# One decode-attention kernel: a V transfer in one piece, eight spare matmuls ahead of each wait for V, and one select for a mask

## The chip, the cores and the metric

The kernel runs on one core of one Trainium2 chip. The metric is the device time of one execution in microseconds (us); where several runs are given, the median counts.

## What is computed

Attention for one query per head: 16 heads, a cache of 8192 positions, 256 numbers each, all in bf16.

```python
B, H, Sq, Sk, D = 1, 16, 1, 8192, 256
scale = q.shape[-1] ** -0.5
scores = jnp.einsum("bhqd,bhkd->bhqk", q, k) * scale
p = _softmax(scores, axis=-1)
return jnp.einsum("bhqk,bhkd->bhqd", p, v)
```

Every number of K and V is used once.

## The kernel before, in words

**Tiles.** Heads go in pairs, eight of them, numbered 0 to 7. Each head takes 64 of the 128 partitions, so a partition holds J = 128 positions of its head. K of a pair is one tile of 128 x 32768 numbers, in two alternating buffers (`kbuf`); V is the same size in a single buffer (`vbuf`). Columns 0 to 63 are the first side of a pair (HJ = 64), the rest the second.

**Transfers.** SyncE issues all loads of K and V, in the order of the list `ORDER` (line 17), through one queue (line 136). A name without a plus is a whole tile, or the first half where `parts` (line 100) says so; with a plus it is the second half. The last V, v7, is cut at columns 64, 92, 112 and 124 (`CUTS`). Before a K transfer into a used buffer SyncE waits until the scores of the pair two before are done (line 125, 126); before a V transfer that ends within the first half it waits for the semaphore `pa`, the first 32 matmuls on the V before, else for `pr`, all of them (line 128). Behind the last piece it waits for its landing (line 139), then writes the outputs out (lines 143, 145).

**Scores.** Of each side's 64 positions GpSimd multiplies 24 with the query, three at a time (line 215), and ScalarE scales and sums them (line 450); VectorE does the other 40 (line 252). ScalarE reports each group of three on the semaphore `sp`: 16 groups (NG) for a pair, and the count starts two ahead.

**Softmax and V.** TensorE's program is a loop of nine passes, h = 0 to 8 (line 356). Pass h first does V of pair h - 1: it waits for the exponentials (`ex`, line 359), then for V (`v`, line 360), and multiplies with V two positions at a time (`doubles`, line 319), 32 matmuls for the first half and 32 for the second, behind a wait for `vb` (line 362); these take turns on two halves of the array's columns. In the last pass the second half stops at position 92: 46 matmuls in all. `total` (line 307) sums the exponentials and raises `pr`. Then pass h turns the maximum of pair h (line 292, a wait for VectorE's `m`), spreads it (line 296), and broadcasts the query of the pair after next (line 283). At its end the old `keep_running` multiplies the fp32 unit matrix by itself four times side by side, 128 x 512 in all, into a bank that nobody reads (line 330); then `gather` (line 341) waits for ScalarE's copy of the accumulator (`cm`, line 423) and joins the parts of pair h - 1.

ScalarE does, within the scores of the following pair, the exponentials (line 409), then the copy (line 423), and after the second side the final scaling (line 430). VectorE takes the maximum (line 234) behind the first side of the following pair.

**The end.** Behind the loop 72 small matmuls (line 384) add positions 92 to 127 of the last pair, in three groups that wait for the pieces of v7 at 92, 112 and 124. Then ScalarE and VectorE scale one half each (lines 471, 272).

**The start.** GpSimd builds the masks: `which`, two rows that are one over their head's 64 columns (one memset and two selects, lines 181 to 183), and `ident`, the unit matrix (lines 187, 188). TensorE needs `which` for its first two matmuls.

Of the kernel before, what the change touches and what calls it, by code (L numbers as in the profile page):

```python
# [5 lines left out]
ALU = mybir.AluOpType  # L6
# [7 lines left out]
GRP = 3  # L14
CH = 8
SIDES = 2
ORDER = "k0 k0+ k1 v0 k2 v1 k3 v2 k4 v3 k5 v4 k6 k6+ k7 v5 v5+ k7+ v6 v6+ v7"
CUTS = (0, 64, 92, 112, 124)
LAST_PAIRED = 92
STRIP = 64  # L20
BLK = 32
ROWS = 98
# [3 lines left out]
def bass_standalone__mha_softmax__decode_kernel(nc: bass.Bass, q: bass.AP, k: bass.AP, v: bass.AP, out: bass.AP):  # L26
    B, H, Sq, D = q.shape
    Sk = k.shape[2]
    P = 128
# [20 lines left out]
    with contextlib.ExitStack() as ctx:  # L50
# [9 lines left out]
        def sem(name):  # L60
            if name not in sems:
                sems[name] = ctx.enter_context(nc.semaphore(name))
            return sems[name]
# [33 lines left out]
        spare = ps("spare", [P, 512])  # L97

        stream = []
        parts = {name: (0, HJ) for name in ("k0", "k6", "k7", "v5", "v6")}  # L100
        for name in ORDER.split():
            kind, n = name[0], int(name[1])
            if name == f"v{LAST}":
# [56 lines left out]
        def _(pool):  # L160
            done = [0]

            def step(ins):
                done[0] += 1
                ins.then_inc(sem("pool"), 1)
                pool.wait_ge(sem("pool"), done[0])

            def keep(t, base, step_p, step_x, op, fill):
                step(
                    pool.affine_select(  # L170
                        out=t[:, :],
                        in_=t[:, :],
                        compare_op=op,
                        fill=fill,
                        base=base,
                        pattern=[[step_x, P]],
                        channel_multiplier=step_p,
                    )
                )

            step(pool.memset(which[:, :], 1.0))
            keep(which, 0, -HP, 1, ALU.is_ge, 0.0)
            keep(which, HP - 1, HP, -1, ALU.is_ge, 0.0)
            pool.nop().then_inc(sem("cb"), 1)
            for name, n in AHEAD.items():
                pool.nop().then_inc(sem(name), n)
            step(pool.memset(ident[:, :], 0.0))
            keep(ident, 0, 1, -1, ALU.not_equal, 1.0)
            step(pool.memset(ones, 1.0))
            step(pool.memset(half[:, :], 1.0))  # L190
            for c in (0, BLK):
# [89 lines left out]
        def _(pe):  # L281
# [45 lines left out]
                return ins  # L327

            def keep_running():
                pe.matmul(  # L330
                    spare[:, :].rearrange("p (b x) -> p b x", x=P),
                    lhsT=ident[:, :],
                    rhs=ident[:, :].rearrange("p (b x) -> p b x", b=1).to_broadcast([P, 512 // P, P]),
                    start=True,
                    stop=True,
                )

            def gather():
                for n in range(2):
# [16 lines left out]
            with pe.Fori(0, NP + 1) as h:  # L356
                par = pe.snap(h % 2)
                with pe.If(h > 0):
                    pe.wait_ge(sem("ex"), h)
                    pe.wait_ge(sem("v"), h * 16)  # L360
                    doubles(0, HJ).then_inc(sem("pa"), 1)
                    pe.wait_ge(sem("vb"), (h // (NP - 2) + h // LAST + h // NP) * 16 + 16)
                    doubles(HJ, LP)
                    with pe.If(h < NP):
                        doubles(LP, J)
                    total(h)
                with pe.If(h < NP):
                    pe.wait_ge(sem("m"), h + 1)
                    turned()
                    pe.wait_ge(sem("g"), h + 1)  # L370
                    spread()
                with pe.If(h < NP - 2):
                    qcast(back(h, -2), par)
                with pe.If(h > 0):
                    keep_running()
                    pe.wait_ge(sem("cm"), h)
                    pe.wait_ge(sem("fin"), h)
                    gather().then_inc(sem("pv"), 1)
# [124 lines left out]
```

## Time and profile before

| | us |
|---|---|
| median of 3 runs | 317.23 (317.05 to 317.38) |
| the profiled execution | 317.37 |
| its span, first to last instruction | 316.1 |
| VectorE busy | 225.6 (71%) |
| GpSimd busy | 209.8 (66%) |
| ScalarE busy | 194.6 (62%) |
| TensorE busy | 107.1 (34%) |
| mean granted TensorE clock | 0.73 of full |
| HBM read | 134.23 MB, 425 GB/s over the span |

The profiled execution has 1.27 us outside its span. Engines are named PE (TensorE matmul), PEld (its weight loads), DVE (VectorE), ACT (ScalarE), POOL (GpSimd), SP (SyncE); a q behind a name is the engine's sequencer. A timeline row holds start, duration, engine, line, operation, the tiles out<-in, the shape and the count, and in brackets the engine's idle time before it and what ended that. A row of a table of stages holds the stage, its length, the busy time and instructions of PE, PEld, DVE, ACT and POOL, the granted clock, the share of the DMA engines and GB/s. A row by line gives the shortest, median and longest duration in ns, and the first and last start.

### The profile page before, as it was taken

Reading aid. Unit: us, or ns where it says so; the run is one execution under the profiler, and the core shown is the slowest. Engines: PE = TensorE matmul, PEld = TensorE weight load, DVE = VectorE, ACT = ScalarE, POOL = GpSimd, SP = SyncE. Lnnn points to the kernel's source line nnn. Section 1 sums busy time; section 2 is a strip of 40 time slices with the busy share of each in tenths; the row PEclk is TensorE's granted clock in tenths of the full one; section 3 lists DMA queues with packets and bytes.
Section 4 is the critical chain, followed back from the end, with each engine's and each line's share of the span. In section 5 each row is a group of like instructions: output and inputs, shape, how many; then the busy total and the mean of one; then the engine's idle time right before and its main releaser. Section 6 shows DMA issues by size and latency. Waiting matters only on the chain.

```text
span 316.1 us, 7081 instructions
## 1 busy us (share of the span) xinstructions
PE 107.1 (34%) x718; PEld 46.8 (15%) x718; DVE 225.6 (71%) x1305; ACT 194.6 (62%) x840; POOL 209.8 (66%) x146
## 2 busy tenths in 40 slices
PE   0000000192005900069000790007700564258678
PEld 0000000041001400024000240002300122113335
DVE  0198989695596946969369692896989698969300
ACT  2066777766278653696537964468677967686541
POOL 3188888875486845858368582786888588868300
PEclk9999999997555785559755588555965558756779
DMA  8999999999999999999999999999999999999996
GB/s 333 402 460 456 473 398 398 489 440 398 398 398 531 398 398 398 531 398 398 489 440 398 398 531 398 398 398 464 398 464 398 464 398 464 398 464 406 456 400 267
DMA packets 3639, 134.25 MB, mean 425 GB/s; under 512 B 406, under 2 KB 438, under 8 KB 694
## 3 DMA queue, kind: packets, MB, share of 16 engines
q1 hardware_dynamic: 3620, 134.23, 98.8%
q8 instruction: 1, 0.02, 0.0%
q10 hardware_dynamic: 18, 0.01, 0.0%
HBM read 134.23 MB, written 0.01 MB: 425 GB/s over the span
## 4 chain that ended last, share of the span: by engine, by line
DMA 51%; POOL 16%; ACT 10%; PE 7%; issue 6%; ACTq 6%; POOLq 3%; SPq 0%
DMA kbuf<-in_k_dram 32%; DMA vbuf<-in_v_dram 19%; POOL prod L215 16%; ACT prod L450 8%; PE acc L319 6%; ACTq L450 4%; POOLq L215 2%; ACTq L446 2%; PE ob L384 1%; ACT E L409 0%; PE spare L330 0%; ACT comb L423 0%; POOLq L214 0%; POOLq L156 0%; POOLq L212 0%
## 5 line engine op out<-in xcount | busy, mean ns | idle before, releaser
L252 DVE SCALAR_TENSOR_TENSOR kbuf<-kbuf,qrow x640 | 219.9, 417 | 65.3 <-issue 65.3
L215 POOL TENSOR_TENSOR prod<-kbuf,q_now 128x768 f32 x128 | 207.0, 1639 | 83.5 <-ACT prod L450 46.3
L450 ACT ACTIVATE prod<-prod x384 | 155.3, 405 | 103.9 <-POOL prod L215 86.9
L319 PE MATMUL acc<-vbuf,E 128*64 128x512 bf16 x494 | 73.3, 468 | 15.7 <-DMA vbuf<-in_v_dram 12.7
L450 ACT ACTIVATION_READ_ACCUMULATOR prod<-prod x384 | 71.6, 186 | 0.0
L292 PE MATMUL mx<-ident,small 128*1 128x128 f32 x16 | 4.5, 380 | 176.2 <-DVE small L234 176.2
L252 DVE DVE_READ_ACCUMULATOR kbuf<-kbuf,qrow x640 | 52.8, 82 | 0.0
L319 PEld LDWEIGHTS acc<-vbuf,E 128*64 128x64 bf16 x494 | 33.0, 134 | 55.5 <-issue 25.8
L292 PEld LDWEIGHTS mx<-ident,small 128*1 128x1 f32 x16 | 0.7, 81 | 177.2 <-DVE small L234 177.2
L409 ACT ACTIVATE E<-S,negb 64x128 bf16 x16 | 13.9, 866 | 1.5 <-ACT negb L404 1.4
L330 PE MATMUL spare<-ident 128*128 128x512 f32 x16 | 14.7, 1016 | 0.1
L341 PE MATMUL ob<-comb,small 98*2 98x128 f32 x64 | 7.3, 373 | 9.9 <-ACT comb L423 9.9
L228 DVE RECIPROCAL small<-tot 34x1 f32 (+1 forms) x8 | 1.3, 159 | 10.8 <-PE tot L307 10.7
L423 ACT ACTIVATE comb<-acc 98x512 f32<-98x512 f32 x8 | 4.7, 593 | 6.2 <-PE tot L307 6.2
L409 ACT ACTIVATION_READ_ACCUMULATOR E<-S,negb 64x1 f32 x16 | 7.9, 494 | 0.0
L238 DVE TENSOR_REDUCE small<-mx 1x2 f32<-1x128 f32 x8 | 2.2, 279 | 7.0 <-PE mx L292 7.0
L341 PEld LDWEIGHTS ob<-comb,small 98*2 98x2 f32 x64 | 2.7, 99 | 22.0 <-ACT comb L423 21.0
L430 ACT ACTIVATE qo<-ob,small 2x128 f32 x14 | 4.9, 352 | 1.0 <-PE ob L341 0.9
L234 DVE TENSOR_REDUCE small<-S 128x1 f32 x8 | 2.3, 281 | 2.8 <-ACT prod L450 2.8
L296 PE MATMUL mx<-small 1*64 1x1 f32 x32 | 2.9, 244 | 3.0 <-DVE small L238 3.0
L330 PEld LDWEIGHTS spare<-ident 128*128 128x128 f32 x16 | 3.6, 279 | 1.4 <-issue 1.3
L283 PE MATMUL qrow<-qo,which 2*128 (+1 forms) x8 | 2.9, 391 | 2.6 <-DMA qo<-in_q_dram 2.4
(25 smaller groups left out, 19.9 us busy)
## 6 DMA issues: line engine op xcount, KB each, us to landing
kbuf<-in_k_dram SPq DMA_DIRECT2D x6, 4096.0 KB, 27.8
vbuf<-in_v_dram SPq DMA_DIRECT2D x5, 4096.0 KB, 23.7
vbuf<-in_v_dram SPq DMA_DIRECT2D x1, 1792.0 KB, 9.0
vbuf<-in_v_dram SPq DMA_DIRECT2D x1, 1280.0 KB, 11.7
vbuf<-in_v_dram SPq DMA_DIRECT2D x1, 768.0 KB, 13.1
vbuf<-in_v_dram SPq DMA_DIRECT2D x1, 256.0 KB, 13.3
kbuf<-in_k_dram SPq DMA_DIRECT2D x5, 44.1
vbuf<-in_v_dram SPq DMA_DIRECT2D x5, 27.9
```

The lines of the kernel that those rows point to most:

```text
L215: pool.tensor_tensor(out=prod[:, b * GRP * D : (b + 1) * GRP * D].rearrange("p (b d) -> p b d", b=GRP), in0=kbuf[:, ds(par * (J * D) + s * ...
L252: ins = dve.scalar_tensor_tensor(out=col, in0=col, scalar=SCALE, in1=qrow[:, ds(par * 512, D)], op0=ALU.mult, op1=ALU.mult, accum_out=S[:, ...
L292: pe.matmul(mx[0:1, 0:P], lhsT=m[:, :], rhs=ident[:, :], start=True, stop=True).then_inc(sem("mT"), 1)
L319: ins = pe.matmul(acc[at : at + STRIP, :], lhsT=E[:, x : x + STRIP], rhs=vbuf[:, j * D : (j + 2) * D], start=(j < 4), stop=(j >= J - 4), s ...
L330: pe.matmul(spare[:, :].rearrange("p (b x) -> p b x", x=P), lhsT=ident[:, :], rhs=ident[:, :].rearrange("p (b x) -> p b x", b=1).to_broadc ...
L341: ins = pe.matmul(ob[row : row + 2, 0:HW], lhsT=sel[:, 2 * n : 2 * n + 2], rhs=comb[:, n * D + a : n * D + a + HW], start=(n == 0), stop=( ...
L384: ins = pe.matmul(ob[row : row + 2, 0:HW], lhsT=E[:, at : at + 2], rhs=vbuf[:, j * D + a : j * D + a + HW], start=False, stop=(j == J - 1) ...
L409: ins = act.activation(out=E[rows, 0 : 2 * J].rearrange("p (b two i t) -> p b i two t", b=J // BLK, two=2, t=2)[:, :, :, :, x], in_=S[rows ...
L423: act.activation(out=comb[:, :], in_=acc[0:ROWS, :], func=ACT.Copy).then_inc(sem("cm"), 1)
L430: ins = act.activation(out=qo[:, ds(i * D + a, HW)], in_=ob[row : row + 2, 0:HW], func=ACT.Copy, scale=recip[row : row + 2, ds(i, 1)],)
L446: with act.Fori(0, SG) as i:
L450: ins = act.activation(out=part, in_=part, func=ACT.Copy, scale=SCALE, accum_out=S[:, ds(par * J + s * HJ + i * GRP + b, 1)],)
```

## The change

Three edits. GpSimd's two masks are built by one helper, a memset and one select each, so `which` takes one select instead of two. The sixth pair's V (pair 5, v5) goes in one transfer: `v5+` leaves the list, `v5` is the whole tile, and TensorE's wait for `vb` no longer counts it. And the spare product, one fp32 matmul ahead of `gather`, becomes a loop of eight bf16 matmuls of 512 columns (the fp32 ones read as pairs of bf16) between the wait for `ex` and that for `v`; in pass 6 TensorE there also waits until ScalarE has summed all groups of pairs 0 to 6.

```diff
-ORDER = "k0 k0+ k1 v0 k2 v1 k3 v2 k4 v3 k5 v4 k6 k6+ k7 v5 v5+ k7+ v6 v6+ v7"
+ORDER = "k0 k0+ k1 v0 k2 v1 k3 v2 k4 v3 k5 v4 k6 k6+ k7 v5 k7+ v6 v6+ v7"
+SPARES = 8
-        parts = {name: (0, HJ) for name in ("k0", "k6", "k7", "v5", "v6")}
+        parts = {name: (0, HJ) for name in ("k0", "k6", "k7", "v6")}
-            def keep(t, base, step_p, step_x, op, fill):
+            def ones_where_zero(t, pattern):
+                step(pool.memset(t[:, :], 0.0))
                 step(
                     pool.affine_select(
...
-            step(pool.memset(which[:, :], 1.0))
-            keep(which, 0, -HP, 1, ALU.is_ge, 0.0)
-            keep(which, HP - 1, HP, -1, ALU.is_ge, 0.0)
+            ones_where_zero(which, [[-1, 2], [0, HP]])
...
-            step(pool.memset(ident[:, :], 0.0))
-            keep(ident, 0, 1, -1, ALU.not_equal, 1.0)
+            ones_where_zero(ident, [[-1, P]])
...
             def keep_running():
-                pe.matmul(
-                    spare[:, :].rearrange("p (b x) -> p b x", x=P),
-                    lhsT=ident[:, :],
-                    rhs=ident[:, :].rearrange("p (b x) -> p b x", b=1).to_broadcast([P, 512 // P, P]),
-                    start=True,
-                    stop=True,
-                )
+                flat = ident[:, :].bitcast(BF16)
+                with pe.Fori(0, SPARES):
+                    pe.matmul(
+                        spare[:, :].rearrange("p (b x) -> p b x", x=2 * P),
+                        lhsT=flat[:, 0:P],
+                        rhs=flat.rearrange("p (b x) -> p b x", b=1).to_broadcast([P, 256 // P, 2 * P]),
+                        start=True,
+                        stop=True,
+                    )
...
                     pe.wait_ge(sem("ex"), h)
+                    with pe.If(h == NP - 2):
+                        pe.wait_ge(sem("sp"), (NP - 1) * NG + 2)
+                    keep_running()
                     pe.wait_ge(sem("v"), h * 16)
                     doubles(0, HJ).then_inc(sem("pa"), 1)
-                    pe.wait_ge(sem("vb"), (h // (NP - 2) + h // LAST + h // NP) * 16 + 16)
+                    pe.wait_ge(sem("vb"), (h // LAST + h // NP) * 16 + 16)
...
                 with pe.If(h > 0):
-                    keep_running()
                     pe.wait_ge(sem("cm"), h)
                     pe.wait_ge(sem("fin"), h)
                     gather().then_inc(sem("pv"), 1)
```

TensorE at the head of a pass of its loop, before: `acc` is the accumulator of the products with V, and the brackets name the semaphores that a row waits for.

```order
L358 COMPARE_AND_BRANCH
L360 REGISTER_ALU [waits ex]
L319 MATMUL acc<-vbuf,E 64x512 [waits v]
L319 MATMUL acc<-vbuf,E 64x512 x31
L362 ISA
L319 MATMUL acc<-vbuf,E 64x512 [waits vb]
```

The same place after:

```order
L359 COMPARE_AND_BRANCH
L361 COMPARE_AND_BRANCH [waits ex]
L361 UNCONDITIONAL_BRANCH [waits sp]
L330 UNCONDITIONAL_BRANCH
L331 MATMUL spare<-ident 128x512
L330 REGISTER_ALU
L330 COMPARE_AND_BRANCH
L364 REGISTER_ALU
L318 MATMUL acc<-vbuf,E 64x512 [waits v]
L318 MATMUL acc<-vbuf,E 64x512 x31
L366 ISA
L318 MATMUL acc<-vbuf,E 64x512 [waits vb]
```

A branch with the wait for `sp` (pass 6 alone takes it) and the loop of spare products now stand between the wait for `ex` and the first row that waits for V; the loop's three rows run eight times.

TensorE at the end of a pass and behind the loop, before: `ob` is the bank of the output rows.

```order
L372 UNCONDITIONAL_BRANCH
L374 COMPARE_AND_BRANCH
L330 MATMUL spare<-ident 128x512
L341 MATMUL ob<-comb,small 2x128 [waits fin,cm]
L341 MATMUL ob<-comb,small 2x128 x3
L374 UNCONDITIONAL_BRANCH
L356 REGISTER_ALU
L356 COMPARE_AND_BRANCH
```

After:

```order
L376 UNCONDITIONAL_BRANCH
L378 COMPARE_AND_BRANCH
L342 MATMUL ob<-comb,small 2x128 [waits fin,cm]
L342 MATMUL ob<-comb,small 2x128 x3
L378 UNCONDITIONAL_BRANCH
L357 REGISTER_ALU
L357 COMPARE_AND_BRANCH
```

The spare product ahead of the gather is gone; all else stands as it stood.

SyncE's transfers from the second half of pair 6's K on, before:

```order
L136 DMA kbuf<-in_k_dram 128x16384
L136 DMA kbuf<-in_k_dram 128x16384 [waits tp,kd]
L136 DMA vbuf<-in_v_dram 128x16384 [waits pa]
L136 DMA vbuf<-in_v_dram 128x16384 [waits pr]
L136 DMA kbuf<-in_k_dram 128x16384
L136 DMA vbuf<-in_v_dram 128x16384 [waits pa]
```

After:

```order
L137 DMA kbuf<-in_k_dram 128x16384
L137 DMA kbuf<-in_k_dram 128x16384 [waits tp,kd]
L137 DMA vbuf<-in_v_dram 128x32768 [waits pr]
L137 DMA kbuf<-in_k_dram 128x16384
L137 DMA vbuf<-in_v_dram 128x16384 [waits pa]
```

The two halves of v5, with a wait for `pa` and one for `pr`, have become one whole transfer that waits for `pr`.

More of the change, by code (lines that the diff above doesn't have):

```diff
@@ L172, in keep @@
                         in_=t[:, :],
[L173 to L177, printed above, removed]
-                    )
-                )
-            step(pool.memset(which[:, :], 1.0))
-            keep(which, 0, -HP, 1, ALU.is_ge, 0.0)
-            keep(which, HP - 1, HP, -1, ALU.is_ge, 0.0)
+                        compare_op=ALU.not_equal,
+                        fill=1.0,
+                        base=0,
+                        pattern=pattern,
+                        channel_multiplier=1,
+                    )
+                )
+            ones_where_zero(which, [[-1, 2], [0, HP]])
             pool.nop().then_inc(sem("cb"), 1)
```

## The prediction

> **What bounds the kernel now.** I read the page first, for the share of the DMA queue, then the chain of waits from 225 us on, then the timelines of single engines, and last the table of stages for the clock that TensorE was granted. The page's queue row:
>
> ```profile
> span 316.1 us, 7081 instructions
> ...
> q1 hardware_dynamic: 3620, 134.23, 98.8%
> ```
>
> All of K and V goes through one queue that moved data in 98.8% of the span. An engine's work matters only where it empties that queue, or behind the last bytes. What lies there is the end of the chain (start, duration, what):
>
> ```profile
> 291.18 12.97 DMA vbuf<-in_v_dram
> ...
> 304.20 6.71 PE acc L319 x46
> 310.91 0.04 PE tot L307 x2
> 310.95 1.05 PE spare L330 x2
> 312.00 0.54 PE ob L341 x8
> 312.54 2.03 PE ob L384 x72
> ```
>
> The last pair's first V half lands at 304.15 us, and from there TensorE works without a gap to 312.54 + 2.03 = 314.57. The queue of SyncE shows when the last V piece had landed, since line 143 stands behind line 139's wait for it:
>
> ```profile
> 314.08 0.32 SPq L143 DMA_DIRECT2D out_dram<-qo  x1
> ```
>
> So the last bytes came at 314.08, and 8 of the 72 matmuls of line 384 need them: 8/72 of 2.03 is 0.23 us, and the last drains in about 0.2. TensorE ends at 314.57, where the data alone would have ended it at about 314.5. Transfer and TensorE are level at the end: TensorE earlier gains under 0.1 us there, later it costs in full.
>
> How fast it is there hangs on its clock. The table of stages (length, busy us and instructions by engine, then the granted clock):
>
> ```profile
> 255.60:259.60 4.00, 3.97 (x20) 1.75 (x22) 4.00 (x25) 2.63 (x13) 3.23 (x2) 0.50 0.91 393
> 259.60:261.20 1.60, 1.60 (x16) 0.62 (x12) 1.60 (x11) 1.31 (x6) 1.40 (x1) 1.00 1.47 635
> 284.80:290.30 5.50, 5.50 (x26) 2.36 (x28) 5.50 (x35) 3.19 (x16) 4.97 (x4) 0.50 1.08 465
> 290.30:293.70 3.40, 0.84 (x8) 0.23 (x4) 3.40 (x21) 2.62 (x12) 2.88 (x2) 1.00 0.90 386
> 294.50:297.10 2.60, 2.60 (x14) 1.14 (x16) 0.00 (x0) 2.31 (x13) 0.86 (x1) 0.50 0.93 403
> 297.10:300.50 3.40, 2.95 (x30) 1.52 (x26) 0.72 (x3) 0.60 (x3) 0.00 (x0) 0.99 1.07 463
> 300.50:304.00 3.50, 1.72 (x10) 0.57 (x10) 0.00 (x0) 2.46 (x6) 0.00 (x0) 1.00 0.94 402
> 304.20:307.40 3.20, 3.20 (x16) 1.46 (x18) 0.00 (x0) 0.60 (x2) 0.00 (x0) 0.50 1.01 430
> 307.40:310.70 3.30, 3.30 (x32) 1.68 (x29) 0.00 (x0) 0.00 (x0) 0.00 (x0) 1.00 0.97 406
> ```
>
> Every burst on V starts at half clock and gets the full one later: 4.0, 5.5, 2.6 and 3.2 us after its start. The rates at both clocks:
>
> ```profile
> 304.20 1.07 PE L319 MATMUL acc<-vbuf,E 128*64 128x512 bf16 x4 [0.35 <-DMA vbuf<-in_v_dram]
> 307.72 1.24 PE L319 MATMUL acc<-vbuf,E 128*64 128x512 bf16 x10
> L319 PE MATMUL acc<-vbuf,E x494: 379/379/637, 63.0 to 310.5; 128*64 128x512 bf16 x165
> ```
>
> These matmuls go in pairs, one on each half of the array's columns. At half clock the second pair starts 1.07 - 0.64 = 0.43 us after the first; at full clock five pairs need four steps and one duration, so a step is (1.24 - 0.38)/4 = 0.215 us.
>
> **The change part by part.** *One select for rows.* GpSimd fills the mask of rows with one select fewer, and the unit matrix comes earlier:
>
> ```profile
> 1.07 0.63 POOL L170 TENSOR_SCALAR_AFFINE_SELECT which<-which 2x128 bf16<-2x128 bf16 x2
> 14.33 3.23 POOL L215 TENSOR_TENSOR prod<-kbuf,q_now 128x768 f32 x2 [9.54 <-issue]
> ```
>
> Half of 0.63 us goes, with GpSimd idle for 9.54 us before its first product at 14.33, which waits for K. Worth 0; without that cover it would be worth 0.3.
>
> *The sixth pair's V whole.* One issue instead of two, and TensorE starts on it when all of it is there. These TensorE rows hold the sixth and seventh pairs:
>
> ```profile
> 255.63 5.59 PE L319 MATMUL acc<-vbuf,E 128*64 128x512 bf16 x32 [4.04 <-DMA vbuf<-in_v_dram]
> 265.34 5.33 PE L319 MATMUL acc<-vbuf,E 128*64 128x512 bf16 x32 [4.12 <-DMA vbuf<-in_v_dram]
> 277.37 0.59 PE L292 MATMUL mx<-ident,small 128*1 128x128 f32 x2 [6.66 <-DVE small L234]
> 284.78 6.37 PE L319 MATMUL acc<-vbuf,E 128*64 128x512 bf16 x32 [0.86 <-DMA vbuf<-in_v_dram]
> 294.48 4.94 PE L319 MATMUL acc<-vbuf,E 128*64 128x512 bf16 x32 [3.34 <-DMA vbuf<-in_v_dram]
> ```
>
> Two halves are 265.34 - 255.63 = 9.71 apart, so 19.42 for both. Whole transfers, from two K landings with four transfers between them:
>
> ```profile
> 75.90 44.08 DMA kbuf<-in_k_dram
> 153.08 44.30 DMA kbuf<-in_k_dram
> ```
>
> (197.38 - 119.98)/4 = 19.35 each: the whole one saves 0.07 us of the queue. Against it stands the late start. The new wait holds TensorE until ScalarE has summed all of pair 6 (counted from 0); its next work there is:
>
> ```profile
> 264.65 0.71 ACT L430 ACTIVATE qo<-ob,small 2x128 f32 x2
> ```
>
> Spare matmuls from about 264.7, at 0.43 each, end at 268.2; nothing else is queued that any engine needs before 277.37, where the maximum is late anyway. But SyncE's issue of the next V half waits for the first 32 matmuls. With the full clock at 2.6 to 5.5 us after 264.7, these end between 271.6 and 272.7. The queue runs dry when the K half ahead lands, 9.71 before 284.78, so at 275.07. The last output transfer, from issue at 314.97 to the end of the span, took under 1.15 us, so the data flows again by 273.9: hidden by 1.2 us, and each us beyond that would cost one.
>
> *The spare matmuls of the other passes.* Eight times 0.43 is 3.4 us ahead of each V. In passes 1 to 5 whole transfers of V are asked for early:
>
> ```profile
> vbuf<-in_v_dram SPq DMA_DIRECT2D x5, 27.9
> ```
>
> 27.9 us from issue to landing, 19.35 of them moving: 8.5 us in hand against 3.4, so nothing. In the seventh pass the burst that began at 284.78 begins up to 3.4 us later, near 288.2, with the full clock by then or soon, and ends between 291.8 and 292.4 instead of at 291.18, where the chain has SyncE's next issue; the queue has work until 284.78 + 9.71 - 0.04, near 294.4. With 1.15 us to flow that is hidden by 0.9 us; nothing again.
>
> *The spare matmuls of the last pass* are on the path. The exponentials are long done there, since TensorE comes from the gather that waits for ScalarE's copy behind them:
>
> ```profile
> 302.59 0.60 ACT L423 ACTIVATE comb<-acc 98x512 f32<-98x512 f32 x1
> 303.24 0.60 PE L341 MATMUL ob<-comb,small 98*2 98x128 f32 x8 [1.58 <-ACT comb L423]
> L356 PEldq ALU_OP  x9: 36/36/36, 60.0 to 311.6; - x9
> L356 PEldq COMPARE_BRANCH  x9: 76/209/217, 60.1 to 311.7; - x9
> 310.98 0.60 ACT L423 ACTIVATE comb<-acc 98x512 f32<-98x512 f32 x1 [6.17 <-PE tot L307]
> 311.93 0.60 PE L341 MATMUL ob<-comb,small 98*2 98x128 f32 x8
> ```
>
> So no hole is filled: the eight stand between 303.84 and a V that is there at 304.15. A loop turn adds 0.04 + 0.21 of sequencer time, under 0.43, so it hides. I start them at 304.2, with a branch more than now. Half clock: the stage row shows it from 304.0 already with the old spare in the hole, and now the hole is empty. No row has eight full-width bf16 matmuls; 512 columns at half clock take 0.43 in the nearest rows. The old fp32 product is the far end, at 2.06 us for two records in 278.72's group:
>
> ```profile
> 278.72 2.06 PE L330 MATMUL spare<-ident 128*128 128x512 f32 x2
> ```
>
> At 1.03 each the eight would cost 4.8 us more; I take 0.43, the same type and columns. Below it stands 0.215 at full clock.
>
> Sum: 304.2 + 8 x 0.43 = 307.64, full clock from about then; 23 pairs have 22 steps of 0.215 and one duration of 0.38, ending at 312.75 against 310.91, so +1.84. The old spare behind the total goes: the gather can start 0.05 after the copy (303.24 against 303.19), so at 311.63 instead of 311.93: -0.30. With -0.07 from the whole V: **+1.47 us**. The profiled execution took 317.37 for a span of 316.1 and lies 0.14 above the median, 317.23; from the median, 317.23 + 1.47 = **318.7 us**.
>
> **The rivals.** *The clock stays full (not slower).* If the spare matmuls of the pass before, or a shorter pause, keep the full clock to 304.2, eight take 8 x 0.215 = 1.72 us, and the burst ends at 305.92 + 4.73 + 0.38 = 311.03: +0.12 - 0.30 - 0.07, which is before the last bytes allow, so 317.2. The point that decides: each us by which the full clock comes before 307.64 gives back half a us, so by 306.0 the loss is under 0.63 us. For it: the pauses at 301.7 and 303.8 are short. Against: the clock fell at 304.0 after just these pauses, and the soonest rise in the rows is 2.6 us into a burst, so 306.8. The Trainium skill, "TensorE: Matmul & The Clock Gate", section "Why this matters for your kernels", says that the clock falls only with idle gaps of over some 3 us between bursts; by that rule this rival would hold. The row of 300.50 to 304.00 disagrees: 1.72 us busy, no gap over 1.6 us, and the next stage is at 0.50. Chance 0.14.
>
> *The clock comes late.* With the rise 5.5 us after 304.2, as in the stage from 284.80, five pairs more run at 0.43: +1.05, so 319.8. The unit matrix, read as bf16, is mostly zeros; did it not count as work, the burst itself would have to earn the clock, up to 320.5. Chance 0.14.
>
> *An early chain.* If the seventh burst leaves the clock full at 294.48, its second half ends 1.1 us sooner, the spares move forward with it, and about 0.7 remain: 318.0. I count it to the forecast.
>
> *The queue runs dry at 275.07*, if the wait and a half clock make the first 32 matmuls end after 274: 1 us for each. Chance 0.04, 319.5.
>
> **How the numbers follow.** Forecast with the early chain 0.65, late clock 0.14, dry queue 0.04: 0.83 slower, of which 0.03 may fall within the bound; full clock 0.14; some gain that no row shows 0.03. A difference of 0.2%, 0.63 us, is what this kernel's runs can tell. Faster by so much would need the last bytes sooner, and 0.07 is all that the transfers give: 0.03. Within: 0.17. Slower: 0.80. The range reaches from 317.1, with the full clock in it, to 319.8.
>
> **What would show it.** Right: eight spare matmuls from about 304.2 at steps of 0.43, clock 0.50 there; the last burst from about 307.6; the gather 0.7 us behind the total; the last bytes still near 314.0, and the last matmuls 1.5 us later than now, all their data waiting for them. Wrong: a clock of 1.00 at 304, or spares that start before 303, or a queue with a gap near 275 or 294.

## The result and the profile after

| | before | changed |
|---|---|---|
| median of 6 runs, us | 317.31 (316.79 to 318.15) | 320.15 (319.64 to 321.42) |
| ratio | | 1.0087 (95%: 1.0061 to 1.0114) |
| profiled execution, us | 317.37 | 320.25 |
| its span, us | 316.1 | 318.8 |

The change makes the kernel 2.84 us slower; 1.47 was forecast. The forecast had the sign and the last pass right; the measured median lies 0.35 us above its range.

First the queue of V and K on the page, and the queue of SyncE from 255 us on, in the changed kernel:

```profile
q1 hardware_dynamic: 3476, 134.23, 98.0%
```

```profile
271.68 30.55 SPq L137 DMA_DIRECT2D vbuf<-in_v_dram  x7
315.12 0.32 SPq L144 DMA_DIRECT2D out_dram<-qo  x1
```

The same two rows of the kernel before (the second stands in the prediction) begin at 261.26 and 314.08. So the first V half of pair 6 is asked for at 271.68, as the prediction had it (271.6 to 272.7), but the last bytes come at 315.12, 1.04 us later than before, where the prediction had them at 314.0. The page's 98.8% of 316.1 us and this 98.0% of 318.8 us are the same work, 312.4 us. Of the 2.7 us that came on top, 1.65 lie behind the last bytes, where the queue has nothing left to do, and 1.04 ahead of them, where it was empty or slow.

TensorE's timeline from the second half of pair 6's V on:

```profile
295.06 5.33 PE L318 MATMUL acc<-vbuf,E 128*64 128x512 bf16 x32 [3.84 <-DMA vbuf<-in_v_dram]
300.23 0.20 PE L306 MATMUL tot<-lsum,half 128*34 128x1 f32 x2
304.20 0.60 PE L342 MATMUL ob<-comb,small 98*2 98x128 f32 x8 [2.82 <-ACT comb L426]
305.20 3.55 PE L331 MATMUL spare<-ident 128*128 128x512 bf16 x8 [0.40 <-issue]
308.69 5.21 PE L318 MATMUL acc<-vbuf,E 128*64 128x512 bf16 x46
313.73 0.20 PE L306 MATMUL tot<-lsum,half 128*34 128x1 f32 x2
314.62 0.60 PE L342 MATMUL ob<-comb,small 98*2 98x128 f32 x8 [0.69 <-ACT comb L426]
315.05 2.18 PE L387 MATMUL ob<-vbuf,E 128*2 128x128 bf16 x72
```

And the table of stages for the same stretch, with the granted clock third from the right:

```profile
295.10:298.60 3.50, 3.50 (x18) 1.58 (x20) 0.29 (x1) 1.92 (x8) 0.00 (x0) 0.51 1.05 449
298.60:300.40 1.80, 1.80 (x21) 0.95 (x16) 0.00 (x0) 0.00 (x0) 0.00 (x0) 1.00 0.85 364
305.20:308.80 3.60, 3.60 (x10) 0.91 (x12) 0.00 (x0) 0.56 (x2) 0.00 (x0) 0.53 1.00 419
308.80:313.90 5.10, 5.10 (x48) 2.62 (x48) 0.00 (x0) 0.00 (x0) 0.00 (x0) 1.00 0.93 383
```

The last pass is what was forecast, moved 1 us to the right. Eight spare matmuls from 305.20 to 308.69 at half clock (3.49 us, forecast 3.44); the burst behind them at full clock (5.04 to the total's start, forecast 4.95); the gather 0.89 behind the total (forecast 0.88). What was not forecast stands ahead of it: the second half of pair 6's V lands at 295.02 instead of 294.44, and its burst gets the full clock 3.5 us after its start instead of 2.7. From burst to total that is 5.17 us instead of 4.78.

So the 2.7 us of the span are the forecast 1.47, and 1.23 more: 0.58 for the late landing, 0.07 that the whole V did not bring to this place, 0.39 for the clock in that burst, and 0.19 in four small differences of the last pass. The clock's share is a matter of phase (see the account of the prediction below). The late landing is the one with a cause to find.

### The profile page after: what moved, and what is told of

It is laid out like the page before. It is cut to its first block, busy times and chain, and to the rows that moved or that the text cites. A ratio compares the mean times of both kernels' runs of the same rounds, so it can differ in the third digit from the quotient of the medians.

```text
span 318.8 us, 7320 instructions
## 1 busy us (share of the span) xinstructions
PE 106.2 (33%) x766; PEld 45.2 (14%) x766; DVE 225.6 (71%) x1305; ACT 194.6 (61%) x840; POOL 209.6 (66%) x145
## 4 chain that ended last, share of the span: by engine, by line
DMA 38%; POOL 18%; ACT 13%; PE 9%; issue 9%; ACTq 9%; POOLq 4%; DVE 0%; SPq 0%
DMA kbuf<-in_k_dram 31%; POOL prod L214 18%; ACT prod L453 11%; DMA vbuf<-in_v_dram 6%; PE acc L318 5%; ACTq L453 5%; POOLq L214 3%; PE spare L331 2%; ACTq L449 2%; ACT comb L426 1%; PE ob L387 1%; ACT E L412 1%; POOLq L213 0%; PE ob L342 0%; POOLq L157 0%
## 5 line engine op out<-in xcount | busy, mean ns | idle before, releaser
L318 PE MATMUL acc<-vbuf,E 128*64 128x512 bf16 x494 | 59.3, 400 | 3.8 <-DMA vbuf<-in_v_dram 3.8
L331 PE MATMUL spare<-ident 128*128 128x512 bf16 x64 | 28.1, 613 | 17.1 <-ACT prod L453 13.5
L318 PEld LDWEIGHTS acc<-vbuf,E 128*64 128x64 bf16 x494 | 28.4, 116 | 35.8 <-issue 9.7
L331 PEld LDWEIGHTS spare<-ident 128*128 128x128 bf16 x64 | 6.6, 104 | 36.5 <-issue 36.5
L407 ACT ACTIVATE negb<-mx 128x1 f32<-128x1 f32 x8 | 1.3, 165 | 4.4 <-PE mx L295 4.3
```

The lines of the kernel that those rows point to most:

```text
L318: ins = pe.matmul(acc[at : at + STRIP, :], lhsT=E[:, x : x + STRIP], rhs=vbuf[:, j * D : (j + 2) * D], start=(j < 4), stop=(j >= J - 4), s ...
L331: pe.matmul(spare[:, :].rearrange("p (b x) -> p b x", x=2 * P), lhsT=flat[:, 0:P], rhs=flat.rearrange("p (b x) -> p b x", b=1).to_broadcas ...
```

## Where the late bytes come from

The trace records the landing of each transfer on each of the 16 DMA engines. The last of the 16, in us, and in brackets how far it lies behind the first:

```
                 K 7, 2nd half   V 6, 1st half   V 6, 2nd half   V 7, 1st half   last piece
before           275.01 (0.34)   284.73 (0.36)   294.44 (0.37)   304.15 (0.35)   314.07 (0.33)
changed          274.38 (0.38)   284.90 (1.18)   295.02 (1.59)   304.92 (1.77)   315.11 (1.58)
```

Up to the K half that lands at 274.38 the changed kernel is 0.63 us ahead, with the engines together. One transfer later the last engine is 0.8 us late, and no engine makes up for that. That transfer is the one that was asked for at 271.68.

The trace also keeps every packet of the queue. Joined where one ends and the next begins, they make 16 rows, one for each engine. Around 274 us 14 of the 16 go from the last packet of the K half to the first of the V half without a hole. The other two have nothing to move for 0.5 and 0.8 us, until 274.44 and 274.56, and their first packets of 32 KB then take 1.64 and 1.42 us instead of 1.22. In the kernel before no engine has such a hole. By the next landing, at 295.02, the last engine has lost 0.4 us more; the trace shows packets of 1.4 and 1.5 us between 291.8 and 294.7 there, and why they were slow stays open.

Two theories stood against each other. **Theory A**: the spare matmuls of the last pass are the whole loss, and the late bytes are an accident of this run. **Theory B**: a V half that is asked for 2.3 to 2.7 us before the queue runs dry comes too late for some of the engines; pass 6, with its wait and its spares, causes it, and the last bytes pay.

## The experiments

Each was timed in five rounds beside the kernel before on the same chip, which had medians of 317.16 to 317.39 us. A ratio is that to the kernel before, with its 95% interval.

**The last pass without spares.** In the changed kernel:

```diff
-                    keep_running()
+                    with pe.If(h < NP):
+                        keep_running()
```

> The changed kernel without the eight spare matmuls in the last pass (h = 8); all other passes keep them. Theory A (the loss is the spare matmuls in front of the last burst, and nothing else): the burst starts when its V lands, the time falls by the whole 2.8 us, to 317.3. Theory B (A, and beside it the next V half is asked for too late in pass 6, at 271.68 us, so that part of the queue runs dry and the last bytes come at 315.1 instead of 314.1): the last bytes still come near 315.1, the time falls only to about 318.3.

319.31 us, ratio 1.0050 (1.0031 to 1.0068). The tail is gone and most of the loss is still there: theory A is out. SyncE's queue and the end of TensorE's timeline:

```profile
272.23 30.71 SPq L137 DMA_DIRECT2D vbuf<-in_v_dram  x7
316.00 0.32 SPq L144 DMA_DIRECT2D out_dram<-qo  x1
```

```profile
312.62 0.20 PE L306 MATMUL tot<-lsum,half 128*34 128x1 f32 x2
313.94 1.29 PE L388 MATMUL ob<-vbuf,E 128*2 128x128 bf16 x40
315.41 1.06 PE L388 MATMUL ob<-vbuf,E 128*2 128x128 bf16 x32 [0.18 <-DMA vbuf<-in_v_dram]
```

Now TensorE waits for V among the last 72 matmuls; the last bytes, at 316.0, end the kernel. It lies 1 us above what theory B said: everything in this execution came later (the K half ahead at 275.05 instead of 274.38), and the last engine lost 1.3 us instead of 0.8, although the request at 272.23 was a little further ahead of that landing, 2.5 to 2.8 us. So the price is not a fixed one for each us of lead.

**Holding the same V half in the kernel before.** One more wait in SyncE's queue, on GpSimd's count of groups, and nothing else:

```diff
+                    if n == NP - 2 and a == 0:
+                        sp.wait_ge(sem("tp"), 117)
```

> The kernel before, with one more wait ahead of the first V half of the seventh pair: SyncE issues it when GpSimd has done five groups of pair 7, near 273.0 us, 2.0 us before the queue would run dry at 275.0. With 1.15 us from issue to flow, as I had put it (theory A), it lands at 284.7 as before and the time is 317.3. Theory B (an issue that comes less than some 2.7 us ahead finds part of the queue empty): it lands 1 to 1.6 us later, and the time is 318.3 to 319.

319.59 us, ratio 1.0074 (1.0048 to 1.0100). With 116 in place of 117:

> The kernel before with one more wait ahead of the first V half of the seventh pair: SyncE issues it after four groups of pair 7, near 270.9 us, 4.1 us before the queue would run dry, instead of 2 us as in the run held to 273. Theory B with 3.2 to 3.5 us from issue to the slowest engine's first bytes: nothing is lost, 317.3. If any hold cost time (a queue that wants to be full for longer), 318 or more.

317.39 us, ratio 0.9996 (0.9979 to 1.0013). The two profiles, SyncE's request and TensorE's burst on the half that was asked for; first held to 273, then to 271:

```profile
273.18 29.95 SPq L138 DMA_DIRECT2D vbuf<-in_v_dram  x7
```

```profile
286.13 5.14 PE L321 MATMUL acc<-vbuf,E 128*64 128x512 bf16 x32 [2.15 <-DMA vbuf<-in_v_dram]
```

```profile
271.13 30.64 SPq L138 DMA_DIRECT2D vbuf<-in_v_dram  x7
```

```profile
284.92 5.58 PE L321 MATMUL acc<-vbuf,E 128*64 128x512 bf16 x32 [0.82 <-DMA vbuf<-in_v_dram]
```

Asked for 3.7 to 4.0 us ahead of the first and the last engine's landing, the half lands as ever; 1.5 to 1.9 us ahead, it lands 1.35 us late. Counted by landings, the slowest engine got going only 3.2 us behind the request (landed at 286.08, less the 9.71 us that a half moves, less 273.18), in the changed kernel 3.5 us (284.90 - 9.71 - 271.68). The packets split that: in the run held to 273 the first packet of the half began 1.1 us behind the request on the earliest engine and 2.3 us on the last, in the changed kernel 2.8 and 2.9 us on the two that had run dry; the rest is slow first packets (1.3 to 2.0 us instead of 1.22) and the time from a packet's end to its landing.

The table of stages shows the empty engines too, if both stages are read together. The rows are the kernel before, the changed one and the two that were held (273, then 271); the last two columns are the DMA share and GB/s:

```profile
271.00:274.00 3.00, 0.00 (x0) 0.00 (x0) 3.00 (x19) 1.86 (x9) 2.58 (x2) 0.88 0.81 350
274.00:276.00 2.00, 0.00 (x0) 0.00 (x0) 2.00 (x13) 1.71 (x9) 1.48 (x2) 0.50 1.22 524
```

```profile
271.00:274.00 3.00, 3.00 (x30) 1.60 (x28) 3.00 (x19) 2.14 (x11) 3.00 (x2) 1.00 1.17 502
274.00:276.00 2.00, 1.13 (x14) 0.57 (x8) 2.00 (x13) 1.52 (x8) 1.48 (x2) 1.00 0.70 295
```

```profile
271.00:274.00 3.00, 0.00 (x0) 0.00 (x0) 3.00 (x19) 1.85 (x10) 2.53 (x2) 1.00 0.81 350
274.00:276.00 2.00, 0.00 (x0) 0.00 (x0) 2.00 (x13) 1.71 (x10) 1.47 (x2) 0.88 0.94 295
```

```profile
271.00:274.00 3.00, 0.00 (x0) 0.00 (x0) 3.00 (x19) 1.85 (x10) 2.48 (x3) 1.00 0.86 371
274.00:276.00 2.00, 0.00 (x0) 0.00 (x0) 2.00 (x13) 1.71 (x10) 1.47 (x2) 0.81 1.22 524
```

Over the five us the kernel before moved 2.10 MB and the one held to 271 2.16 MB, but the one held to 273 only 1.64 MB. The changed kernel moved 2.10 MB as well: its 295 stands behind a 502, and holes on two of 16 engines are too small for this table. There the packets show them.

The same reading of the other requests narrows the point that decides. Where the engines lay within 0.8 us of one another, a request up to 2.81 us ahead of the first landing left a hole of 0.3 us or more on some engine in each of the traces, and one at least 2.84 us ahead left none; the kernel before itself asks for pair 7's V at 291.18, 2.89 us ahead, and loses nothing. Where the engines had drawn apart, requests 3.2 and 3.3 us ahead could still leave holes (0.6 us in pass 7 of the run held to 273).

**Each part alone.** The whole V, in the kernel before, with nothing else of the change:

```diff
-ORDER = "k0 k0+ k1 v0 k2 v1 k3 v2 k4 v3 k5 v4 k6 k6+ k7 v5 v5+ k7+ v6 v6+ v7"
+ORDER = "k0 k0+ k1 v0 k2 v1 k3 v2 k4 v3 k5 v4 k6 k6+ k7 v5 k7+ v6 v6+ v7"
...
-        parts = {name: (0, HJ) for name in ("k0", "k6", "k7", "v5", "v6")}
+        parts = {name: (0, HJ) for name in ("k0", "k6", "k7", "v6")}
...
-                    pe.wait_ge(sem("vb"), (h // (NP - 2) + h // LAST + h // NP) * 16 + 16)
+                    pe.wait_ge(sem("vb"), (h // LAST + h // NP) * 16 + 16)
```

> The kernel before with the sixth pair's V in one transfer, and nothing else. Theories A and B: the transfer saves 0.07 us, TensorE starts the burst at 265.3 at half clock and SyncE asks for the next V half near 270.5: 317.1 to 317.3, no difference that can be measured. If the whole transfer itself were the cause of the late bytes, the last bytes come near 315 and the time near 318.3.

317.28 us, ratio 0.9998 (0.9981 to 1.0015): free, as forecast. TensorE started at 264.73 and the next half was asked for at 270.39, 3.7 us before the K half ahead landed, and nothing was lost:

```profile
264.73 9.09 PE L319 MATMUL acc<-vbuf,E 128*64 128x512 bf16 x64 [13.70 <-DMA vbuf<-in_v_dram]
270.39 31.70 SPq L136 DMA_DIRECT2D vbuf<-in_v_dram  x7
```

Then the wait and the spares of pass 6 alone, with the whole V and the old spare product in all passes. This run and the next were made from the changed kernel, so they have its one select as well. Their diffs are told against the kernel before; `keep_eight` stands in all diffs for the loop of eight bf16 matmuls, whose definition is left out:

```diff
                     pe.wait_ge(sem("ex"), h)
+                    with pe.If(h == NP - 2):
+                        pe.wait_ge(sem("sp"), (NP - 1) * NG + 2)
+                        keep_eight()
```

> The kernel before with V of pair 5 whole, and in pass 6 alone the wait for ScalarE's sums and the eight spare matmuls ahead of V; the old spare product stays in every pass. This is the late request by itself: the next V half is asked for near 271.7. Theory B: its landing slips by 0.8 to 1.4 us, the last bytes come at 315 to 316, the time is 318.2 to 319.3. Theory A: no difference, 317.3.

319.47 us, ratio 1.0086 (1.0056 to 1.0116). That this is the late request alone is not shown. Its profiled execution, the fastest of its runs, took 318.31, asked at 272.66 and had the last bytes at 314.94. But one engine was already 1.6 us behind the first from 82 us on (the section on the build has the cause), and that engine lost nothing at the late request: it landed the K half at 275.56 and the V half at 285.27, 9.71 us later.

And the spares of the last pass alone, in the kernel before, V in halves, no spare product elsewhere:

```diff
                     pe.wait_ge(sem("ex"), h)
+                    with pe.If(h == NP):
+                        keep_eight()
...
-                    keep_running()
                     pe.wait_ge(sem("cm"), h)
```

> The kernel before with the eight spare matmuls ahead of V in the last pass alone, no spare product elsewhere, and V of pair 5 in halves. This is the tail by itself: the next V half is asked for near 261, the queue stays full, the last bytes come near 314. By theory B the tail alone costs what the prediction's sum gave, 1.5 to 1.8 us: 318.8 to 319.2. By theory A (the tail is the whole loss) it costs 2.8: 320.1.

319.05 us, ratio 1.0056 (1.0035 to 1.0076), so 1.66 us: the forecast sum for the tail was 1.84 - 0.30 = 1.54. The profiled execution took 320.32, 1.27 above the median. In it the clock came late twice: the burst on the second half of pair 6's V took 6.19 us, from 294.01, and the last burst 5.61. SyncE's queue and TensorE:

```profile
260.34 41.68 SPq L137 DMA_DIRECT2D vbuf<-in_v_dram  x7
313.58 0.32 SPq L144 DMA_DIRECT2D out_dram<-qo  x1
```

```profile
304.96 3.59 PE L331 MATMUL spare<-ident 128*128 128x512 bf16 x8
308.48 5.61 PE L318 MATMUL acc<-vbuf,E 128*64 128x512 bf16 x46
313.92 0.20 PE L306 MATMUL tot<-lsum,half 128*34 128x1 f32 x2
315.25 2.18 PE L386 MATMUL ob<-vbuf,E 128*2 128x128 bf16 x72
```

Asked for early, the last bytes are there at 313.6, and all 72 last matmuls run behind them: here TensorE ends the kernel, with no byte late. The two losses do not add (1.66 here, 2.21 with the late request alone in the run held to 273, 2.84 together). In the changed kernel's trace it is TensorE that ends last, at 317.23, and its last matmuls wait for no byte; what the late request adds there is the later start of the last pass.

**Pass 6 without spares.** Two runs meant to take only pass 6's spares away. In the first the condition was written for pass 7 where the last pass, 8, was meant, so that it had none in pass 6 and none in the last pass:

```diff
-                    keep_running()
+                    with pe.If(h < NP - 2):
+                        keep_running()
+                    with pe.If(h == LAST):
+                        keep_running()
```

> The changed kernel without the eight spare matmuls in pass 6 (its wait for ScalarE's sums stays); the last pass keeps them. Theory A: pass 6 is hidden, the time stays at 320.1. Theory B: the first 32 matmuls of pass 6 start at 264.7 instead of 268.0, SyncE asks for the next V half near 270.3 instead of 271.7, the queue stays full, the second half of pair 6's V lands near 293.8 instead of 295.0 and the last bytes near 313.5 to 314.1; the time is 318.6 to 319.0.

319.95 us, ratio 1.0086 (1.0054 to 1.0118). So this is the changed kernel with spares in passes 1 to 5 and 7 alone, and it still loses 2.6 us. Its next half was asked for at 273.30, for two reasons: pair 5's V landed at 266.32 instead of 264.68, with one engine 1.6 us behind the first, and the burst on it began at half clock. The second kept them in the last pass:

```diff
-                    with pe.If(h == LAST):
+                    with pe.If(h > NP - 2):
```

> The changed kernel without the eight spare matmuls in pass 6 alone; the last pass keeps them (the earlier run of this name left them out of the last pass too). The first 32 matmuls of pass 6 now start at 264.7 at half clock, so the next V half is asked for between 270.4 and 271.6, hanging on when the full clock comes. Theory B: the loss of the queue shrinks from 0.8 us to between 0 and 0.8, and the tail's 1.5 to 1.8 us stay: 318.9 to 319.9. Theory A: 320.1.

322.29 us, ratio 1.0125 (1.0082 to 1.0168): worse than the changed kernel, outside what either theory gave. It asked at 272.07. The bursts of pass 6 in the two runs:

```profile
266.77 9.95 PE L318 MATMUL acc<-vbuf,E 128*64 128x512 bf16 x64 [14.04 <-DMA vbuf<-in_v_dram]
```

```profile
266.45 9.03 PE L318 MATMUL acc<-vbuf,E 128*64 128x512 bf16 x64 [14.04 <-DMA vbuf<-in_v_dram]
```

Both begin 1.7 us or more behind the 264.73 of the whole V alone, since one engine brought that V late, so neither run tells what the spares of pass 6 cost; without them and without that engine the request came at 270.39 (the whole V alone). The profiled execution of the second run, 322.37, is 2.2 us behind the changed kernel's at its last gather: 0.45 for the later V half, 1.07 for a clock that came later in the burst on it, 0.36 between the gather, at half clock here, and the spares, and 0.32 in the last burst.

**Smaller transfers.** If the 3.2 us were the time to set up one large transfer, a cut V half would flow sooner. The half in four transfers of 16 positions, in the kernel that held it to 273 and in the changed one:

```diff
+            elif name == f"v{NP - 2}":
+                for a in range(0, HJ, 16):
+                    stream.append((kind, n, a, a + 16, "v"))
...
-                    pe.wait_ge(sem("v"), h * 16)
+                    pe.wait_ge(sem("v"), h * 16 + h // LAST * 48)
```

> The run that held the next V half to 273 us, with that half cut into four transfers of 16 positions. If the 3.2 us from issue to the slowest engine's first bytes grow with what one transfer holds (theory B1), the first piece flows after about a quarter of it and little is lost: 317.4 to 317.9. If they are there for any transfer of V (theory B2), it costs as before: 319 to 319.6.

> The changed kernel with the next V half (first half of pair 6's V) in four transfers of 16 positions, asked for at the same time, near 271.7 us. Theory B1: the queue does not run empty, the last bytes come near 314, and the time is the tail's alone: 318.8 to 319.2. Theory B2: as the changed kernel, 320.1.

319.62 us, ratio 1.0074 (1.0047 to 1.0101), the same as uncut; and 321.21 us, ratio 1.0109 (1.0074 to 1.0144), no better than the change. The first piece was asked for at 273.51 and 272.09, and its first packet on the last engine began 1.8 and 3.0 us later, where uncut it was 2.3 and 2.9. So a quarter of the transfer does not clearly shorten the delay: it is 0.5 us less in one and no less in the other.

**The clock at no cost.** The rival with a full clock was tried where the spares hide: in the kernel before, eight in pass 7 in the hole ahead of the gather, and none behind the last total.

```diff
-                    keep_running()
+                    with pe.If(h == LAST):
+                        keep_eight()
+                    with pe.If(h < LAST):
+                        keep_running()
```

> The kernel before with the eight spare matmuls where they hide: in pass 7 at the place of the old spare product, in the 2.7 us in which TensorE waits for the exponentials and the copy; no spare product behind the last total. If the clock follows from that, the last burst begins at full clock and its total comes 1 to 1.5 us sooner, but the last bytes come at 314.1 all the same: 317.3, no difference that can be measured. If TensorE were what ends the kernel, 316 to 316.5.

The stages of its spares, its gather and its last burst:

```profile
301.50:304.70 3.20, 3.07 (x8) 0.76 (x8) 0.00 (x0) 2.34 (x5) 0.00 (x0) 1.00 0.99 412
304.70:306.00 1.30, 0.71 (x10) 0.42 (x12) 0.00 (x0) 0.22 (x1) 0.00 (x0) 1.00 0.98 419
306.00:311.00 5.00, 5.00 (x48) 2.72 (x46) 0.00 (x0) 0.50 (x2) 0.00 (x0) 1.00 0.99 419
```

```profile
313.95 1.06 PE L398 MATMUL ob<-vbuf,E 128*2 128x128 bf16 x32 [0.46 <-DMA vbuf<-in_v_dram]
```

The burst ran at full clock from its start, and TensorE then waited for the last bytes, which came at 314.54, 0.47 us later than in the kernel before. Without that wait it would have ended near 314.4 (72 matmuls of 2.18 us from 312.20) instead of 314.55: a full clock has next to nothing to win here. But the time was 318.32 us, ratio 1.0039 (1.0018 to 1.0060), and 317.3 was expected. That opened a third question.

## A cost of the build, in part settled

Five runs looked for it. The loop of eight in TensorE's program behind the spreading of the maximum, under a condition that never holds, so that it never runs:

```diff
                 with pe.If(h < NP):
...
                     spread()
+                    with pe.If(h == NP):
+                        keep_eight()
```

> The kernel before with the loop of eight spare matmuls standing in TensorE's program behind the spreading of the maximum, under a condition that never holds: it is never run. If the loss of 1.07 us of the spares in the hole comes from the code that stands there (theory C: more program to fetch, which disturbs a transfer near 66 us), it costs again about 1: 318.3. If it comes from running the matmuls, 317.3.

319.16 us, ratio 1.0060 (1.0038 to 1.0082): the build with a loop that is never run is 2 us slower. Its TensorE rows for the turned maxima of the first two pairs, and below them those of the kernel before:

```profile
58.32 0.59 PE L292 MATMUL mx<-ident,small 128*1 128x128 f32 x2 [54.96 <-DVE small L234]
...
98.44 0.58 PE L292 MATMUL mx<-ident,small 128*1 128x128 f32 x2 [26.37 <-DVE small L234]
```

```profile
58.30 0.58 PE L292 MATMUL mx<-ident,small 128*1 128x128 f32 x2 [55.26 <-DVE small L234]
...
96.88 0.59 PE L292 MATMUL mx<-ident,small 128*1 128x128 f32 x2 [24.05 <-DVE small L234]
```

Level at 58, it is 1.56 us late at 98. By the landings K of pair 2 came at 82.65 with one engine 1.73 us behind the first, against 81.09 and 0.44, and the engines stayed that far apart until 295.82. The same eight written out without a loop, in every pass at the old place:

```diff
             def keep_running():
...
+                for _ in range(8):
...
```

> The kernel before with the old spare product replaced, in every pass at its old place, by eight bf16 matmuls written out one behind the other, without a loop or a branch. Behind the last total they stand on the path: 8 x 0.215 = 1.7 us in place of 1.05, so about 0.4 to 0.7 by TensorE's chain: 317.7 to 318.0. If a loop as such cost about 1 us more (theory D), nothing is added here; if the matmuls or the longer program did (theory C), 318.7 or more.

318.42 us, ratio 1.0044 (1.0029 to 1.0059), above what the longer tail explains, so it does not take a loop. And the kernel before without the old product behind the last total:

```diff
-                    keep_running()
+                    with pe.If(h < NP):
+                        keep_running()
```

> The kernel before without the old spare product behind the last total: the other edit of the run with the spares in the hole, alone. TensorE's chain ends 0.3 us sooner at the total, the last bytes decide: 317.2 to 317.3. If this edit were what cost 1.07 us there, 318.3.

317.26 us, ratio 0.9999 (0.9990 to 1.0008): taking that one away costs nothing. Then a shorter program, and the loop run once ahead of all passes:

```diff
                 with pe.If(h > 0):
-                    keep_running()
                     pe.wait_ge(sem("cm"), h)
```

> The kernel before without any spare product: TensorE's program is one matmul shorter in each pass and nothing is added. The clock may come later in the bursts, all hidden but the last. If a longer program is what costs (theory C), nothing is lost here: 316.8 to 317.5. If the bursts needed the spares, 317.8 or more.

```diff
             pe.wait_ge(sem("cf"), 1)
+            keep_eight()
```

> The kernel before with the loop of eight spare matmuls run once ahead of the first pass, near 5 us, when TensorE has nothing to do until 58 us. The program is as long as with the loop that is never run, but the body of the passes is unchanged. If it is code inside the passes that costs (theory C1), 317.2; if any longer program does, or one that lies otherwise in memory (theory C2), 318.2 to 319.2.

318.46 us, ratio 1.0035 (1.0018 to 1.0053), for the shorter one; 317.31 us, ratio 1.0004 (0.9985 to 1.0023), for the longer one. So a longer program is not it either. The run without any spares took between 316.90 and 319.53; its fastest, which is the profiled one, had all engines within 0.6 us and the last bytes at 313.5; the slow ones left no trace. The profiled run with the loop in front took 319.58 although its median is 317.31; there one engine fell 1.2 us back before K of pair 3 landed, and one 1.2 us before the last pieces of V.

What the engine does in that time, the traces do record. The page of each run has a row beside the queue of K and V, here that of the loop that is never run:

```profile
q8 instruction: 1, 0.02, 0.0%
```

It is one packet of 16 KB of instructions, and it travels on one of the 16 engines that bring K and V. That engine's packets, in us, first in the run with the loop that is never run, then in the one with the loop ahead of the passes:

```
K or V to 63.85     instructions 63.85 to 64.78      K or V from 64.77 to 67.68
K or V to 106.80    instructions 106.81 to 107.74    K or V from 107.72 to 110.64
```

The engine loses 0.93 us to the packet and about 0.5 more because its next packet takes 2.91 us instead of 2.42. In seven of the 18 profiled executions this packet comes early, at 63.2 to 65.7 or at 106.8 us, each time between two packets of the engine that then stays 1.0 to 1.5 us behind all others: both runs without spares in pass 6, the spares in pass 6 alone, the spares in the hole, the loop that is never run, the written-out eight, the loop ahead. In the other eleven it comes at 312.7 to 316.9 us, about 1 us into the last 72 matmuls, when hardly anything is left to bring. So what was looked for is this packet. Open is what moves it: one trace of each build cannot say whether a build always has it early, and whose program it brings is not recorded. The loop ahead of the passes had it early in its profiled execution and a median of 317.31 all the same.

The losses near 300 us are something else: the run with the loop ahead and the one without the product behind the last total asked for pair 7's later pieces 2.1 and 2.5 us ahead of the landing before them, and have holes of 1.4 and 0.7 us there, late requests once more.

The packet comes at 316.13 in the changed kernel, behind the last bytes, so its 2.7 us are told by the tail and the late request without it. It is late too in the runs on which theory B rests: no spares in the last pass, both holds, the whole V alone, the last pass's spares alone, and both with smaller transfers. From the others no size of the late request is taken.

## Why the prediction was right and wrong

- **The last pass (right).** Spares on the path at half clock, 8 x 0.43, the burst behind them at full clock, the old product's 0.30 given back: each within 0.1 us of the trace, and 1.66 us alone against 1.54. That it is so close is in part luck: see the clock below.
- **The whole V (right).** Free: 317.28 alone; the 0.07 us is below what can be measured. That the select costs nothing was argued from its cover and not tried alone.
- **The late request (wrong, and the step that failed).** The prediction put 1.15 us from issue to flow, by the last output transfer, and called the request at 271.6 to 272.7 hidden by 1.2 us. The request came at 271.68. But that row is a transfer of 1 KB on an idle queue. Of a V half, the first packet began at most 1.1 us behind the request on the earliest engine (held to 273), but 2.3 us on the last, and 2.8 and 2.9 us on the two that ran dry in the changed kernel; counted by landings 3.2 to 3.5 us were lost. The price, 1 us for each us late, was given, with a chance of 0.04: the mechanism was named and its bound mis-sized, by taking the one row at hand as an upper bound, for 16 engines as for one. The point that decides lies near 2.8 us of lead where the engines lie together, not at 1.15. The request of the seventh pass, at 291.27 and 2.2 us ahead of the first engine's landing, fell under the same wrong bound: one engine has a hole of 0.5 us there.
- **What it cost.** 0.58 us at the second half of pair 6's V, which moved the whole last pass. I had priced it at the last bytes alone; these came 1.04 us late and cost nothing in this execution, since TensorE ended 2.1 us behind them.
- **The clock.** The prediction let the burst before the last stand as it was. Its rise came 3.5 us in instead of 2.7: 0.39 us. Such a burst's rise lay 2.6 to 5.5 us in by the rows of before, so this belonged to the range. In all 18 traces the granted clock changes only on a grid of 3.41 us, whose phase differs from one execution to the next: near the end at 293.74, 297.15, 303.98 and 307.39 in the kernel before, at 295.19, 298.61, 305.43 and 308.85 in the changed one. How far into a burst the rise falls is therefore luck, and so is it that the half clock, 305.43 to 308.85, covered just the eight spares. In the run with the last pass's spares alone it was 302.61 to 309.44, and the last burst took 5.61 us instead of 5.21.
- **The rule of the Trainium skill** ("TensorE: Matmul & The Clock Gate", "Why this matters for your kernels") that asks for no idle gaps over some 3 us between bursts: in the changed kernel the gap ahead of the spares, between the spread at 301.11 and the gather at 304.20, was 2.82 us, and the stage of the spares ran at 0.53. So gaps under 3 us were not enough. That work in the gap keeps the clock is not shown: with eight matmuls in that hole it stayed at 1.00, but with the old product there it fell at 303.98 in the kernel before and stayed full from 299.12 to 316.18 in the run held to 271, whose TensorE program is the same. In the four traces with the eight on the path of the last pass, and that hole empty, the clock fell each time, as the forecast had it.

The version that is best among all that ran is the kernel before; the whole V alone, the hold to 271 and the one without the product behind the last total cannot be told from it.

## What to carry to other kernels

A transfer queue that is the bound must be fed well before it runs dry: here requests up to 2.8 us ahead already left engines empty, and one 3.7 us ahead did not, nor the 2.9 us of the kernel before. So a wait that is moved or added has to be followed to every request that stands behind it, and the lead of that request, not its mere order, is the number to check, with a row of the same kind of transfer and for the slowest engine. Instruction transfers in the trace belong in the same check: they use the same engines. Work that warms an engine's clock pays only where the engine idles anyway and where what it speeds up is what ends last; ahead of a wait that is already over it is a delay.

## What the runs showed of the hardware that was not expected

- From the issue of a 4 MB V half to its first packet passed at most 1.1 us on the earliest of the 16 engines and 2.3 us on the last (held to 273), and 2.8 and 2.9 us on the two that ran dry in the changed kernel; cutting the half into four gave 1.8 and 3.0 us for the last. The Trainium skill, "DMA: Bandwidth & Descriptors", "Latency and other measured facts", gives about 0.6 us to the first byte for such queues; no engine here can be shown to need so little, and the last ones needed about four to five times that.
- Engines that fall behind do not catch up while the queue is full: 0.8 us lost at 274 us was still there, and more, at 315.
- One packet of 16 KB of instructions, on one of the 16 engines, holds up that engine's K and V for 0.9 to 1.1 us, and its next packet takes 2.91 us instead of 2.42; it came near 64 us in some builds and behind 312 in others.
- The granted clock changed only on a grid of 3.41 us in all 18 traces, at a phase of each execution's own.
